# Weight conversion in 512-column pieces, in place, and an FFN that begins at attention step 34

## The chip, the cores and the metric

The kernel runs on one core of one Trainium2 chip. The metric is the device time of one execution in microseconds (us), the median of several runs. The engines are TensorE (PE in the profile; PEld are its weight loads), VectorE (DVE), ScalarE (ACT), GpSimd (POOL) and SyncE (SP), which issues all DMAs here. Each engine works through its own instructions in a fixed order; semaphores tie the engines together.

## The reference

Block-causal attention (8 batches, 8 heads, 576 tokens, head size 64, blocks of 64), then a feed-forward layer over the 4608 tokens:

```python
scores = scale * np.matmul(q, k.transpose(0, 1, 3, 2))
scores = np.where(block_i >= block_j, scores, -1000000000.0)
scores = scores - np.max(scores, axis=-1, keepdims=True)
attn = np.exp(scores)
attn = attn / (np.sum(attn, axis=-1, keepdims=True) + 1e-09)
x = np.matmul(attn, v)                    # then (tokens, heads * head size) = (4608, 512)
h = x @ w_in                              # (4608, 2048)
g = np.where(h >= 1, h, np.where(h <= -1, 0.0, (h + 1) ** 2 / 4))
out = g @ w_out                           # (4608, 512)
```

Queries, keys and values are float32. [...]

## The kernel before

**Numbers.** A float32 operand is split into hi (float32r) and lo = x - hi; a product is hi\*hi + hi\*lo + lo\*hi in float32r passes. Attention times values of batch 0 runs unsplit ("plain").

**Weights.** `convert` (L139) turns a piece of 128 rows of a weight into float32 and splits it. Here a piece has CW = 256 columns, so a weight makes 32 pieces and both make 64. The piece's bits are loaded as pairs of 32-bit words (L147), lower word first. ACT scales the upper word, read as float32 with a step of two words, into the dense tile `work` (L152), and converts the lower word in place (L153). DVE clamps (L154), shifts (L157) and merges the sign (L160), all on the dense `work`. That was the first step; in the second, POOL adds the lower word (L166) and ACT casts to hi (L168); in the third, POOL subtracts hi to get lo (L170). LAG = 2 names those two further steps. Pieces of w_in land in `wih` and `wil`, which stay on chip; pieces of w_out land in `ws`, and when a row block of 512 columns is full it is written to `wo_split` in DRAM, from which the FFN later loads `wo`. `ws` and `wo` share two buffers of the tag "wo". The tiles `bits` and `work` have three buffers each; every other piece below BORROW = 32 uses the FFN's tags "t" and "gl" instead, two buffers each.

**Attention.** 32 pairs of heads (batch by batch, 4 pairs each) run as a software pipeline of eight steps a pair (`attention_steps`, L517): scores by row tiles, softmax (DVE maximum L368, ACT exponential L372, DVE scaling L378; for the last query block L392, L398, L404, in the fourth step), transposes of the probabilities (L418, copied out by L408 and L410), products with the values (L445). An old pair's last products stand in the first two steps of the next one.

**FFN.** Nine chunks of 512 tokens, 16 blocks fc of hidden columns each: 144 units of two half units. `ffn_in` does 12 matmuls into `ph` (L591), then ACT (L600), DVE (L601, L604), ACT (L605) and POOL (L606), and loads `wo`; `ffn_out` does 12 matmuls into `po` (L615, L620).

**The order.** The loop at the end (L659) sets it. At every attention step it starts as many pieces as `want` says: until START = 36 steps a share of EARLY = 24, then more, so that 40 are spread over 24 steps. From START on each attention step is followed by a half unit of the FFN. What is left of the FFN runs after the attention. A scheduler then orders each engine's instructions by their dependencies and a cost model, so that neighbours in the program can stand some places apart on an engine. The memory pools decide how many pieces can be under way.

Of the kernel before, what the change touches and what calls it, by code (L numbers as in the profile page):

```python
# [23 lines left out]
def block_attn_then_ffn(  # L24
# [15 lines left out]
    NTL = S // P                 # whole 128-row tiles of a head  # L40
    SM = NTL * P                 # rows in whole tiles
    QW = SM + 2 * BLK            # query columns of a head: the last block is padded to 128
# [3 lines left out]
    TCH = 512                    # tokens per FFN chunk  # L46
    NCH = NT // TCH
    NTT = TCH // P
    RING = 3 * TCH               # columns of x kept on chip
    G0 = 256                     # query columns of the first attn*v group  # L50
# [4 lines left out]
    BORROW = 32                  # weight pieces among which every other one is converted in  # L55
                                 # buffers of the FFN
    CW = 256                     # columns of a weight that are converted at a time
    F32_TOP = float.fromhex("0x1.dffffcp-96")  # keeps the rounded value finite
    KA = D + NTL                 # contraction rows of hi*hi and the mask
# [7 lines left out]
    conv = ctx.enter_context(tc.tile_pool(name="conv", bufs=3))  # L67
    conv2 = ctx.enter_context(tc.tile_pool(name="conv2", bufs=3))
# [7 lines left out]
    def work_bank(name):  # L76
        # the accumulators' banks serve the attention until the FFN begins
        banks["n"] += 1
        if banks["free"] and banks["n"] % 2:
            return ps_o.tile([P, 512], F32, tag="po", name=name)  # L80
        return ps_w.tile([P, 512], F32, tag="work", name=name)

# [9 lines left out]
    wih = const.tile([P, NCC, DF], F32R, tag="wih", name="wih")  # L92
    wil = const.tile([P, NCC, DF], F32R, tag="wil", name="wil")
    wo_split = dram.tile([NFC, P, 2, DM], F32, tag="wo_split", name="wo_split")

    # Two heads' transposed queries and keys. a: hi rows, then one mask row per whole tile;
    # b: queries hi over lo, keys lo over hi.
# [5 lines left out]
    def last_blocks(t_):  # L103
        """Both heads' last blocks; in the query tiles, head 1's lies behind a block of zeros."""
# [6 lines left out]
    # mask row t: 1 at query block 2t, MASKED at key block 2t + 1  # L111
# [27 lines left out]
    def convert(n, source, hi, lo, done):  # L139
        """CW float64 values, given as bits: their float32, rounded to nearest, in two parts."""  # L140
        if n < BORROW and n % 2:  # in buffers of the FFN
            bits = ffn.tile([P, CW, 2], I32, tag="t", name="bits")
            work = ffn.tile([P, 2, CW], F32, tag="gl", name="work")
        else:
            bits = conv.tile([P, CW, 2], I32, tag="bits", name="bits")
            work = conv2.tile([P, 2, CW], F32, tag="work", name="work")
        nc.sync.dma_start(bits, source.bitcast(I32).rearrange("p (n t) -> p n t", t=2))  # L147
        top, mag = work[:, 0, :], work[:, 1, :].bitcast(U32)
        low = bits[:, :, 0]
        # The upper word, read as float32, has the upper 8 of the 11 exponent bits as its exponent:  # L150
        # times 2^-112 it has the exponent in float32's bias (nothing below 2^-119, and held in range).
        nc.scalar.mul(top, bits[:, :, 1].bitcast(F32), 2.0**-112)  # L152
# [21 lines left out]
    def weight_pieces():  # L174
        """For each piece: its bits, where its parts go, and what follows."""
        for f0 in range(0, DF, CW):
            fs = slice(f0, f0 + CW)
            for cc in range(NCC):
                yield (
                    w_in[cc * P : (cc + 1) * P, fs],  # L180
                    lambda cc=cc, fs=fs: wih[:, cc, fs], lambda cc=cc, fs=fs: wil[:, cc, fs], None,
                )
            for fc in range(f0 // P, (f0 + CW) // P):
                ws = {}

                def part(w, d0, ws=ws):
                    if not ws:
                        ws[0] = ffn.tile([P, 2, DM], F32R, tag="wo", name="ws")
                    return ws[0][:, w, d0 : d0 + CW]

                for d0 in range(0, DM, CW):
                    yield (
                        w_out[fc * P : (fc + 1) * P, d0 : d0 + CW],
                        lambda p_=part, d0=d0: p_(0, d0), lambda p_=part, d0=d0: p_(1, d0),
                        None if d0 + CW < DM else
                        lambda fc=fc, ws=ws: nc.sync.dma_start(wo_split[fc], ws[0].bitcast(F32)),
                    )
# [508 lines left out]
```

## Time and profile before

| what | value |
|---|---|
| median of 3 runs | 1313.78 us (1313.12 to 1313.95) |
| span of the profiled execution | 1305.9 us |
| PE busy | 1234.2 us (95%) |
| DVE busy | 877.9 us (67%) |
| ACT busy | 767.2 us (59%) |
| POOL busy | 462.9 us (35%) |
| mean granted PE clock | 0.978 |

The span runs from the first to the last instruction; the runs' time includes some 8 us around it. The shares are means over the whole span, which has parts of different kinds; so the prediction reads windows of it. In a row of a group, `x` is the count, then follow the busy time in us, the mean of one in ns, and the idle time of the engine just before, with what ended it.

### The profile page before, as it was taken

Reading aid. Unit: us, or ns where it says so; the run is one execution under the profiler, and the core shown is the slowest. Engines: PE = TensorE matmul, PEld = TensorE weight load, DVE = VectorE, ACT = ScalarE, POOL = GpSimd, SP = SyncE. Lnnn points to the kernel's source line nnn. Section 1 sums busy time; section 2 is a strip of 40 time slices with the busy share of each in tenths; the row PEclk is TensorE's granted clock in tenths of the full one; section 3 lists DMA queues with packets and bytes.
Section 4 is the critical chain, followed back from the end, with each engine's and each line's share of the span. In section 5 each row is a group of like instructions: output and inputs, shape, how many; then the busy total and the mean of one; then the engine's idle time right before and its main releaser. Section 6 shows DMA issues by size and latency. Waiting matters only on the chain.

```text
span 1305.9 us, 19727 instructions
## 1 busy us (share of the span) xinstructions
PE 1234.2 (95%) x6496; PEld 1038.7 (80%) x6496; DVE 877.9 (67%) x2200; ACT 767.2 (59%) x1855; POOL 462.9 (35%) x466
## 2 busy tenths in 40 slices
PE   5878777899999999999999999999999999999998
PEld 4666666688888888888888888888888888888886
DVE  8998989867666777776766766676667676322222
ACT  6887676666666666666666666666666565222222
POOL 3554756632233333323333333322333332222221
PEclk9888898999999999999999999999999999999999
DMA  5655454434333433343333432343334322322322
GB/s 153 186 154 167 160 194 159 156 117 131 108 93 104 140 104 97 104 141 106 107 94 103 141 108 85 106 128 104 103 98 137 108 85 63 126 97 97 129 97 97
DMA packets 113766, 156.26 MB, mean 120 GB/s; under 512 B 55920, under 2 KB 72304, under 8 KB 113664
## 3 DMA queue, kind: packets, MB, share of 16 engines
q1 hardware_dynamic: 113664, 155.01, 38.1%
q8 instruction: 51, 0.84, 0.3%
q14 instruction: 51, 0.42, 0.1%
HBM read 120.59 MB, written 17.83 MB: 106 GB/s over the span
## 4 chain that ended last, share of the span: by engine, by line
PE 74%; DVE 12%; ACT 7%; issue 3%; POOL 1%; DMA 1%; SPq 0%; ACTq 0%; POOLq 0%; DVEq 0%
PE ph L591 28%; PE po L615 16%; PE po L620 8%; PE ps_av L445 7%; PE ps_t L418 5%; PE ps_s L345 3%; PE ps_s L348 3%; PE ps_qk L303 3%; DVE pr L378 2%; ACT pr L372 2%; ACT qb L307 2%; DVE nm L368 2%; DVE work L160 1%; DVE work L154 1%; DVE work L157 1%
## 5 line engine op out<-in xcount | busy, mean ns | idle before, releaser
L606 POOL TENSOR_TENSOR gl<-t,gh 128x512 fp32r<-128x512 f32 x144 | 189.6, 1317 | 617.1 <-ACT gh L605 476.0
L615 PE MATMUL po<-wo,gh 128*128 128x512 f32 x1152 | 298.0, 401 | 0.1
L591 PE MATMUL ph<-xh,wih 128*128 128x512 f32 x576 | 240.0, 417 | 1.0 <-DVE sm L354 1.0
L615 PEld LDWEIGHTS po<-wo,gh 128*128 128x128 f32 x1152 | 208.9, 189 | 39.7 <-ACT gh L605 0.5
L601 DVE SCALAR_TENSOR_TENSOR t<-t 128x512 f32<-128x512 f32 x144 | 108.6, 754 | 186.4 <-ACT t L600 186.3
L591 PE MATMUL ph<-xh,wil 128*128 128x512 f32 x576 | 230.7, 401 | 0.0
L591 PE MATMUL ph<-xl,wih 128*128 128x512 f32 x576 | 228.6, 397 | 0.0
L600 ACT ACTIVATE t<-ph 128x512 f32<-128x512 f32 x144 | 86.1, 598 | 167.1 <-PE ph L591 167.1
L372 ACT ACTIVATE pr<-ps_s,nm 128x128 f32<-128x128 f32 (+3 forms) x256 | 134.2, 530 | 58.3 <-DVE nm L368 58.2
L368 DVE TENSOR_REDUCE nm<-ps_s 128x1 f32<-128x128 f32 (+3 forms) x256 | 123.6, 485 | 60.2 <-PE ps_s L348 59.0
L620 PE MATMUL po<-wo,gl 128*128 128x512 f32 x576 | 155.3, 391 | 0.0
L345 PE MATMUL ps_s<-ka,qa 68*128 68x288 f32 (+4 forms) x384 | 124.7, 339 | 21.1 <-ACT pr L372 11.7
L408 ACT CAST pb<-ps_t 128x512 fp32r<-128x512 f32 (+1 forms) x140 | 77.9, 556 | 105.3 <-PE ps_t L418 81.8
L605 ACT CAST gh<-t 128x512 fp32r<-128x512 f32 x144 | 90.2, 626 | 82.3 <-DVE t L604 80.1
L591 PEld LDWEIGHTS ph<-xh,wil 128*128 128x128 f32 x576 | 110.1, 191 | 23.7
L591 PEld LDWEIGHTS ph<-xh,wih 128*128 128x128 f32 x576 | 110.3, 192 | 21.2 <-DVE sm L354 1.5
L591 PEld LDWEIGHTS ph<-xl,wih 128*128 128x128 f32 x576 | 110.9, 192 | 20.5 <-DVE xl L481 0.2
L620 PEld LDWEIGHTS po<-wo,gl 128*128 128x128 f32 x576 | 108.5, 188 | 23.2
L410 DVE TENSOR_TENSOR pb<-ps_t,pb 128x512 fp32r<-128x512 f32 (+1 forms) x140 | 88.3, 631 | 51.1 <-ACT pb L408 51.1
L348 PE MATMUL ps_s<-kb,qb 128*128 128x288 f32 (+4 forms) x384 | 122.3, 325 | 0.0
L418 PE MATMUL ps_t<-ident_r,pr 128*128 128x128 f32 x640 | 108.6, 286 | 7.0 <-DVE x L468 2.2
L378 DVE TENSOR_SCALAR pr<-pr,sm 128x128 f32<-128x128 f32 (+3 forms) x256 | 109.5, 450 | 3.6
(89 smaller groups left out, 2022.2 us busy)
## 6 DMA issues: line engine op xcount, KB each, us to landing
wo<-wo_split SPq DMA_DIRECT2D x144, 512.0 KB, 3.2
out_dram<-ob SPq DMA_DIRECT2D x36, 256.0 KB, 4.5
qn<-in_q_dram SPq DMA_DIRECT2D x32, 256.0 KB, 2.8
kn<-in_k_dram SPq DMA_DIRECT2D x32, 256.0 KB, 2.9
bits<-in_moe_w_in_dram SPq DMA_DIRECT2D x32, 256.0 KB, 2.8
bits<-in_moe_w_out_dram SPq DMA_DIRECT2D x32, 256.0 KB, 2.9
wo_split<-ws SPq DMA_DIRECT2D x16, 512.0 KB, 2.9
qa<-qb SPq DMA_DIRECT2D x63, 128.0 KB, 2.2
```

The lines of the kernel that those rows point to most:

```text
L345: nc.tensor.matmul(ps, qa[:KA, j, c0 : c0 + P], ka[:KA, j, k0 : k0 + n], start=first, stop=False)
L348: nc.tensor.matmul(ps, qb[:, j, c0 : c0 + P], kb[:, j, k0 : k0 + n], start=False, stop=last)
L368: nc.vector.tensor_reduce(out=nm[:, i : i + 1], in_=ps[:, cs], axis=AX.X, op=ALU.max, negate=True)
L372: nc.scalar.activation(pr[:, cs], ps[:, cs], AF.Exp, bias=nm[:, i : i + 1], scale=1.0, accum_out=sm[:, i : i + 1],)
L378: nc.vector.tensor_scalar_mul(pr[:, cs], pr[:, cs], sm[:, i : i + 1])
L418: nc.tensor.transpose(ps[:, c0 : c0 + P], pr[:, c0 : c0 + P], ident)
L445: nc.tensor.matmul(ps[:, lo_col:], vt, x, start=first and i == 0 and m == 0, stop=last and i == len(parts) - 1 and m == len(mov) - 1,)
L591: nc.tensor.matmul(ph, w[:, cc, fs], x[:, cc, xs], start=(cc == 0 and i == 0), stop=(cc == NCC - 1 and i == 2),)
L601: nc.vector.scalar_tensor_tensor(out=t_, in0=t_, scalar=1.0, in1=t_, op0=ALU.min, op1=ALU.mult)
L606: nc.gpsimd.tensor_tensor(out=gl, in0=t_, in1=gh.bitcast(F32), op=ALU.subtract)
L615: nc.tensor.matmul(po[tt], gh[:, ts_], wo[:, w, :], start=(fc == 0 and w == 0), stop=False)
L620: nc.tensor.matmul(po[tt], gl[:, ts_], wo[:, 0, :], start=False, stop=fc == NFC - 1)
```

## The change

A piece has 512 columns, so that both weights make 32 pieces. The upper word is scaled, clamped and kept in `bits`, with a step of two words, and the shifted word goes to a dense tile `mag`. `conv` has two buffers of `bits` and of `mag`, and a pool `early` has two more of each, used by every other piece. w_in is kept in four pairs of tiles of 512 columns; the last pair lies in a pool that is opened in the room of `early` when piece 24 is reached, from which point on only the two `conv` buffers serve. 12 pieces are begun before step 34, then one per step. The FFN begins at step 34 in place of 36. The output tiles `ob` use `conv`'s tags. Comments were taken out as well.

```diff
-    CW = 256                     # columns of a weight that are converted at a time
+    CW = 512
+    NG = DF // CW
...
-    conv = ctx.enter_context(tc.tile_pool(name="conv", bufs=3))
-    conv2 = ctx.enter_context(tc.tile_pool(name="conv2", bufs=3))
+    conv = ctx.enter_context(tc.tile_pool(name="conv", bufs=2))
...
-    wih = const.tile([P, NCC, DF], F32R, tag="wih", name="wih")
-    wil = const.tile([P, NCC, DF], F32R, tag="wil", name="wil")
+    w_in_parts = [
+        [const.tile([P, NCC, CW], F32R, tag=f"wi{x}{g}", name=f"wi{x}{g}") for x in "hl"]
+        for g in range(NG - 1)
+    ]
+    late = {"pool": ctx.enter_context(ExitStack())}
+    late["early"] = late["pool"].enter_context(tc.tile_pool(name="early", bufs=2))
+
+    def open_last_group():
+        late["pool"].close()
+        late["early"] = None
+        last = ctx.enter_context(tc.tile_pool(name="last", bufs=1))
+        w_in_parts.append(
+            [last.tile([P, NCC, CW], F32R, tag=f"wi{x}", name=f"wi{x}") for x in "hl"]
+        )
...
     def convert(n, source, hi, lo, done):
-        if n < BORROW and n % 2:  # in buffers of the FFN
-            bits = ffn.tile([P, CW, 2], I32, tag="t", name="bits")
-            work = ffn.tile([P, 2, CW], F32, tag="gl", name="work")
-        else:
-            bits = conv.tile([P, CW, 2], I32, tag="bits", name="bits")
-            work = conv2.tile([P, 2, CW], F32, tag="work", name="work")
+        pool = late["early"] if n % 2 and late["early"] else conv
+        bits = pool.tile([P, CW, 2], I32, tag="bits", name="bits")
+        mag = pool.tile([P, CW], U32, tag="mag", name="mag")
         nc.sync.dma_start(bits, source.bitcast(I32).rearrange("p (n t) -> p n t", t=2))
-        top, mag = work[:, 0, :], work[:, 1, :].bitcast(U32)
-        low = bits[:, :, 0]
-        nc.scalar.mul(top, bits[:, :, 1].bitcast(F32), 2.0**-112)
+        top, low = bits[:, :, 1].bitcast(F32), bits[:, :, 0]
+        nc.scalar.mul(top, top, 2.0**-112)
         nc.scalar.mul(low, low.bitcast(U32), 2.0**-29)
...
     def weight_pieces():
-        for f0 in range(0, DF, CW):
-            fs = slice(f0, f0 + CW)
+        for g in range(NG):
+            if g == NG - 1:
+                open_last_group()
...
     def ffn_in(c, fc):
-        fs = slice(fc * P, (fc + 1) * P)
+        g, f0 = divmod(fc * P, CW)
+        fs = slice(f0, f0 + P)
+        wih, wil = w_in_parts[g]
...
-            ob = conv.tile([P, DM], F32, tag="bits", name="ob") if tt % 2 else conv2.tile(
-                [P, DM], F32, tag="work", name="ob"
-            )
+            ob = conv.tile([P, DM], F32, tag="bits" if tt % 2 else "mag", name="ob")
...
-    START = 8 * NPAIR + 4        # attention steps before the FFN
-    EARLY = 24                   # conversions before the FFN
+    START = 8 * NPAIR + 2
+    EARLY = 12
...
-        if i < START:
-            want = (i + 1) * EARLY // START
-        else:
-            want = max(
-                EARLY + (i - START + 1) * (NFC // GROUP * PART - EARLY) // (2 * NFC - 4 * GROUP),
-                ((i - START) // (2 * GROUP) + 1) * PART,
-            )
+        want = (i + 1) * EARLY // START if i < START else EARLY + i - START + 1
         want += LAG
```

The pieces come in the same kind of order as before, now by groups of 512 columns of w_in: four pieces of w_in, then the four row blocks of w_out that belong to them. A piece of w_out now fills a whole `ws`.

Two places show how the engines' orders move. First DVE, where the last piece is converted; the names are the program's (`pa`, `pb` are transposed probabilities with their number, `nm` and `sm` the softmax's maximum and sum, `qs`, `ks` the split queries and keys of the next pair). Before, in the fourth step of the eighth pair:

```order
L160 SCALAR_TENSOR_TENSOR work<-work 128x256
L266 SCALAR_TENSOR_TENSOR qs<-qn,qs 128x9x64
L601 SCALAR_TENSOR_TENSOR t<-t 128x512
L368 TENSOR_REDUCE nm<-ps_s 128x1
L604 TENSOR_TENSOR t<-ph,t 128x512
L410 TENSOR_TENSOR pa_3002<-ps_t,pa_3001 128x384
L354 TENSOR_SCALAR sm<-sm 128x1
L275 CAST ks<-kn 128x64
L355 RECIPROCAL sm<-sm 128x1
L378 TENSOR_SCALAR pr<-pr,sm 128x512
L392 TENSOR_REDUCE nm<-ps_s 128x1 x2
L396 TENSOR_TENSOR nm<-nm 128x1
```

Now, in the fourth step of the seventh pair (L162, L165, L168 are the old L154, L157, L160; L403, L411, L610 the old L396, L404, L601):

```order
L165 TENSOR_SCALAR mag<-bits 128x512
L403 TENSOR_TENSOR nm<-nm 128x1
L417 TENSOR_TENSOR pb_2289<-ps_t,pb_2288 128x3x128
L168 SCALAR_TENSOR_TENSOR mag<-bits,mag 128x512
L409 TENSOR_TENSOR sm<-sm 128x1
L361 TENSOR_SCALAR sm<-sm 128x1
L362 RECIPROCAL sm<-sm 128x1
L411 TENSOR_SCALAR pr<-pr,sm 128x576
L610 SCALAR_TENSOR_TENSOR t<-t 128x512
```

The last conversion stands one pair of heads, eight steps, earlier in the program; 12 FFN units' L601 stand ahead of it before, 9 of L610 now.

Second POOL, among the later pieces (`vs` are split values, `gl` is the FFN's lo part). Before:

```order
L166 TENSOR_TENSOR work<-work,bits 128x256
L170 TENSOR_TENSOR ws<-work,ws 128x256 x2
L166 TENSOR_TENSOR work<-work,bits 128x256 x2
L170 TENSOR_TENSOR ws<-work,ws 128x256 x2
L170 TENSOR_TENSOR wil<-work,wih 128x256
L606 TENSOR_TENSOR gl<-t,gh 128x512
```

Now, in the last group (L174 and L178 are the old L166 and L170, L615 the old L606):

```order
L174 TENSOR_TENSOR mag<-mag,bits 128x512
L615 TENSOR_TENSOR gl<-t,gh 128x512
L178 TENSOR_TENSOR wil<-mag,wih 128x512
L174 TENSOR_TENSOR mag<-mag,bits 128x512
L299 TENSOR_TENSOR vs_2293<-vn,vs_2293 128x4x64
L299 TENSOR_TENSOR vs_2293<-vn,vs_2293 64x64
L178 TENSOR_TENSOR wil<-mag,wih 128x512
```

Adds of two pieces no longer stand side by side here: with two buffers, an add is followed by the subtraction of the piece before it.

More of the change, by code (lines that the diff above doesn't have):

```diff
@@ L54, in block_attn_then_ffn @@
     EPS = 1e-9
-    BORROW = 32
-    CW = 256
+    CW = 512
+    NG = DF // CW
     F32_TOP = float.fromhex("0x1.dffffcp-96")
@@ L174, in weight_pieces, with part @@
     def weight_pieces():
-        for f0 in range(0, DF, CW):
-            fs = slice(f0, f0 + CW)
+        for g in range(NG):
+            if g == NG - 1:
+                open_last_group()
             for cc in range(NCC):
                 yield (
-                    w_in[cc * P : (cc + 1) * P, fs],
-                    lambda cc=cc, fs=fs: wih[:, cc, fs], lambda cc=cc, fs=fs: wil[:, cc, fs], None,
+                    w_in[cc * P : (cc + 1) * P, g * CW : (g + 1) * CW],
+                    *(lambda cc=cc, part=part: part[:, cc, :] for part in w_in_parts[g]), None,
                 )
-            for fc in range(f0 // P, (f0 + CW) // P):
+            for fc in range(g * CW // P, (g + 1) * CW // P):
                 ws = {}
-                def part(w, d0, ws=ws):
+                def part(w, ws=ws):
                     if not ws:
                         ws[0] = ffn.tile([P, 2, DM], F32R, tag="wo", name="ws")
[L189 to L196, printed above, removed]
-                    )
+                    return ws[0][:, w, :]
+                yield (
+                    w_out[fc * P : (fc + 1) * P, :],
+                    lambda p_=part: p_(0), lambda p_=part: p_(1),
+                    lambda fc=fc, ws=ws: nc.sync.dma_start(wo_split[fc], ws[0].bitcast(F32)),
+                )
     def prepare_weights():
@@ L647, in feed_forward @@
         yield
-    START = 8 * NPAIR + 4
-    GROUP = CW // P
-    PART = NCC + GROUP * DM // CW
-    EARLY = 24
+    START = 8 * NPAIR + 2
+    EARLY = 12
     LAG = 2
@@ L659, in block_attn_then_ffn @@
     for i, _ in enumerate(attention_steps()):
-        if i < START:
-            want = (i + 1) * EARLY // START
-        else:
-            want = max(
-                EARLY + (i - START + 1) * (NFC // GROUP * PART - EARLY) // (2 * NFC - 4 * GROUP),
-                ((i - START) // (2 * GROUP) + 1) * PART,
-            )
+        want = (i + 1) * EARLY // START if i < START else EARLY + i - START + 1
         want += LAG
```

## Prediction

> **What bounds the kernel now.** I read the 40 slices first, then the windows, then the groups of each engine in two stretches.
>
> ```profile
> span 1305.9 us, 19727 instructions
> ...
> PE   5878777899999999999999999999999999999998
> ...
> DVE  8998989867666777776766766676667676322222
> PEclk9888898999999999999999999999999999999999
> ...
> 0.00:105.00 105.00, 76.53 (x404) 61.99 (x404) 91.22 (x272) 82.94 (x226) 49.54 (x67) 0.92 0.56 164
> 105.00:258.00 153.00, 121.85 (x571) 96.85 (x571) 138.92 (x319) 103.53 (x281) 97.21 (x111) 0.89 0.51 166
> 258.00:1105.00 847.00, 840.31 (x4654) 718.59 (x4654) 592.09 (x1527) 531.57 (x1267) 269.33 (x252) 1.00 0.36 109
> ...
> 1105.00:1205.00 100.00, 100.00 (x453) 82.95 (x453) 29.60 (x48) 26.40 (x47) 23.66 (x19) 1.00 0.29 100
> ```
>
> The window rows give the busy time of PE, weight load, DVE, ACT and POOL, then PE's clock. There are two regimes. From 258 us on PE is busy 99% and more: nothing that other engines save there counts. Up to 258 us, where the last weight piece is converted, DVE is busy 230.1 of 258 us (0.892), PE has gaps and a granted clock of about 0.9. The change lies in this first regime, and what it is worth is the time by which the regime ends sooner, less the PE work that it then leaves over.
>
> ```profile
> L160 DVE SCALAR_TENSOR_TENSOR work<-work 128x256 uint32<-128x256 uint32 x64 | 34.9, 550 | 0.5
> L154 DVE TENSOR_SCALAR work<-work 128x256 f32<-128x256 f32 x64 | 29.4, 464 | 7.9 <-ACT work L152 7.7
> L157 DVE TENSOR_SCALAR work<-work 128x256 uint32<-128x256 uint32 x64 | 27.7, 440 | 0.5
> L378 DVE TENSOR_SCALAR pr<-pr,sm 128x512 f32<-128x512 f32 x14 | 12.0, 854 | 0.1
> L601 DVE SCALAR_TENSOR_TENSOR t<-t 128x512 f32<-128x512 f32 x12 | 11.2, 936 | 0.6 <-ACT t L600 0.5
> L378 DVE TENSOR_SCALAR pr<-pr,sm 128x384 f32<-128x384 f32 x15 | 10.8, 717 | 0.1
> ...
> L378 DVE TENSOR_SCALAR pr<-pr,sm 128x256 f32<-128x256 f32 x15 | 8.3, 555 | 0.0
> ...
> L378 DVE TENSOR_SCALAR pr<-pr,sm 128x128 f32<-128x128 f32 x15 | 7.7, 515 | 0.1
> L604 DVE TENSOR_TENSOR t<-ph,t 128x512 f32<-128x512 f32 x11 | 7.5, 679 | 0.0
> ```
>
> These are DVE's groups of 0 to 258 us (busy us, mean ns). Conversion takes 92.0 us of DVE, all else 138.1. The same forms from 300 to 1100 us, where POOL does little, are shorter:
>
> ```profile
> L601 DVE SCALAR_TENSOR_TENSOR t<-t 128x512 f32<-128x512 f32 x93 | 70.1, 754 | 52.5 <-ACT t L600 52.5
> ...
> L378 DVE TENSOR_SCALAR pr<-pr,sm 128x512 f32<-128x512 f32 x46 | 22.0, 479 | 0.8
> ...
> L378 DVE TENSOR_SCALAR pr<-pr,sm 128x384 f32<-128x384 f32 x46 | 19.1, 415 | 0.8
> ...
> L378 DVE TENSOR_SCALAR pr<-pr,sm 128x256 f32<-128x256 f32 x46 | 16.0, 347 | 0.0
> ...
> L378 DVE TENSOR_SCALAR pr<-pr,sm 128x128 f32<-128x128 f32 x46 | 13.1, 284 | 1.4
> ```
>
> So beside a busy POOL a DVE instruction on SBUF is held up: 854 for 479 ns, 936 for 754.
>
> **Part 1, wider pieces on DVE.** Two old pieces cost 2 x (550 + 464 + 440) = 2908 ns. A new one has three instructions of 512 columns. A tensor_scalar gains 132 ns from 256 to 512 columns without POOL (479 - 347) and 299 beside it (854 - 555): L154 becomes 596 to 763, L157 572 to 739; I take the middles, 680 and 655. The third lies between 754 and 936; I take 880, nearer the row of this stretch. Sum 2.22 us, ends 1.92 and 2.44: 32 pieces take 71.0 us for 92.0.
>
> **Part 2, longer POOL instructions.** POOL's conversion groups up to 262 us:
>
> ```profile
> L166 POOL TENSOR_TENSOR work<-work,bits 128x256 int32<-128x256 int32 x64 | 53.4, 838 | 66.5 <-DVE work L160 11.3 <-ACT bits L153 9.5 <-ACT pr L372 7.9
> L170 POOL TENSOR_TENSOR wil<-work,wih 128x256 fp32r<-128x256 f32 x32 | 27.1, 848 | 8.8 <-ACT wih L168 8.2 <-DMA vn<-in_v_dram 0.5
> ...
> L606 POOL TENSOR_TENSOR gl<-t,gh 128x512 fp32r<-128x512 f32 x12 | 16.6, 1381 | 17.4 <-ACT gh L605 15.6 <-DMA kn<-in_k_dram 1.5 <-DVE work L154 0.2
> ```
>
> At 512 columns one lasts as L606's 1381 ns: 64 make 88 us where 128 made 106. POOL is busier with each and less in total. The attention's scaling (L378) is held (854 - 479) x 14 + (717 - 415 + 555 - 347 + 515 - 284) x 15 = 16.4 us in this stretch. If waits follow the length of a POOL instruction (1381/840, 1.6 times) this grows by 10 us; if they follow POOL's total they grow by nothing. I take 6. [...] The rows agree that DVE is held (854 for 479 ns), not how the hold grows.
>
> **Part 3, where the conversions end.** The first pair of rows on DVE's order, in the part on the change, shows it: before, the last conversion stands in the fourth step of the eighth pair, with 12 FFN units (L601) ahead; now in the fourth step of the seventh, with 9 ahead. So conversion ends 8 attention steps and 3 FFN units (6 half units) sooner in the program: this comes from the denser schedule, one piece of 512 columns a step for 40/24 x 256, and from the start two steps earlier, which moves the FFN's first unit, its matmuls, its two DVE instructions and its wo load on SP, ahead of two attention steps. What leaves the DVE-bound stretch:
>
> ```profile
> L160 DVE SCALAR_TENSOR_TENSOR work<-work 128x256 uint32<-128x256 uint32 x40 | 23.1, 586 | 0.4
> L157 DVE TENSOR_SCALAR work<-work 128x256 uint32<-128x256 uint32 x39 | 19.8, 516 | 0.3
> ...
> L154 DVE TENSOR_SCALAR work<-work 128x256 f32<-128x256 f32 x39 | 17.1, 446 | 1.7 <-ACT work L152 1.6
> ```
>
> From 105 to 258 us (24 steps) DVE spends 138.9 - 60.0 = 78.9 us beside conversion, of it 12 x (936 + 679) ns = 19.4 on FFN units and 59.5 on attention, 2.48 a step. Eight steps are 19.8 us, three units 4.8. The stretch then holds 138.1 - 24.6 = 113.5, + 71.0, + 6 = 190.5 us of DVE; at 0.892 it ends at 213.6, 44.4 us sooner.
>
> What PE must still do comes back on the path. The last-block activations mark the pairs:
>
> ```profile
> L398 ACT ACTIVATE pr<-ps_s,nm x50: 492/503/512, 262.7 to 1094.2; 128x288 f32<-128x288 f32 x50
> ```
>
> Two a pair, 25 pairs: 831.5/24 = 34.6 us for 8 steps with 8 half units. A half unit is 12 matmuls, 12 x 100/453 = 2.65 us. Eight steps and six halves are 34.6 - 5.3 = 29.3 us. **Sum:** -44.4 + 29.3 = -15.1 us. On the profiled span that is 1290.8; 7.9 us lie between the span and the median of 1313.78, so 1298.7. With 1.92 us and no more waits it is 1281, with 2.44 and 10 it is 1311.
>
> **Part 4, at nothing.** ACT's conversion instructions and the loads halve in number; both lie behind DVE (ACT is busy 186 of 258 us), and without that cover less ACT work could only gain. The last group's tiles lie where the early buffers were, so the first cast of the 25th piece waits for POOL's subtraction of the 24th: once, at most one POOL instruction, 1.4 us, with the softmax behind it on ACT. Output tiles have two and two buffers for three and three; a chunk needs four and comes every 16 x 2 half units, 85 us at 2.65 each, so they are free.
>
> **Rivals.** *Strided DVE (slower).* The upper word stays in bits, so DVE reads every second word in all three instructions and writes so in one. No DVE row has a step of two. The nearest has a step of four, against a dense one:
>
> ```profile
> L309 DVE CAST qa<-ps_qk x1: 1046/1046/1046, 10.9 to 10.9; 64x512 fp32r<-64x512 f32 x1
> L309 DVE CAST ka<-ps_qk x1: 1084/1084/1084, 12.0 to 12.0; 64x512 fp32r<-64x512 f32 x1
> ...
> L630 DVE COPY ob<-po 128x512 f32<-128x512 f32 x12 | 8.2, 685 | 1.4 <-PE po L620 1.4
> ...
> L152 ACT ACTIVATE work<-bits 128x256 f32<-128x256 f32 x64 | 28.0, 439 | 13.6 <-DMA bits<-in_moe_w_in_dram 8.0 <-POOL ws L170 4.3 <-DMA bits<-in_moe_w_out_dram 1.3
> L153 ACT ACTIVATE bits<-bits 128x256 int32<-128x256 uint32 x64 | 27.9, 444 | 1.0 <-DMA bits<-in_moe_w_in_dram 0.5 <-DMA bits<-in_moe_w_out_dram 0.4
> ...
> L168 ACT CAST wih<-work 128x256 fp32r<-128x256 f32 x32 | 12.9, 409 | 17.5 <-POOL work L166 17.3
> ...
> L307 ACT CAST kb<-ps_qk 128x512 fp32r<-128x512 f32 x16 | 17.8, 1114 | 0.3 <-PE ps_qk L303 0.3
> ...
> L408 ACT CAST pb<-ps_t 128x512 fp32r<-128x512 f32 x9 | 5.4, 602 | 1.3 <-PE ps_t L432 1.3
> ```
>
> Step four costs DVE 380 ns (mean 1065 - 685). At that price three instructions add 1.14 us a piece, 36.5 us, 41 on the path: 1340. At half of it 1319. The midpoint, 0.85 us a piece, gives 1329; from 0.42 us a piece on (15.1 x 0.892/32) the change is no gain. Against it: on ACT step four (L307) costs 512 ns over L408, but step two (L152, L153) only 30 to 35 over L168, and POOL's L166, with one operand of step two, is no longer than L170. I keep step two at nothing in the sum. [...]
>
> *Buffers (about the same).* After 24 pieces only two bits buffers are left, and ws shares two wo buffers with the FFN's wo, now with four ws in a row. POOL's rows on the change show the result: one piece's add (L174) stands between subtractions (L178), where before two adds often stood together.
>
> ```profile
> wo<-wo_split SPq DMA_DIRECT2D x144, 512.0 KB, 3.2
> ```
>
> A piece holds its bits for a landing of this size, 3.2 us, two ACT passes of at most 2 x 2 x 0.44, 2.2 of DVE and 1.38 of POOL: 8.5 us. Two buffers pass one piece per 4.3 us, and a step takes 153/24 = 6.4. If queueing doubles the 8.5, each of the last 8 pieces comes 2.1 us late, 17 us in all; behind its load on SP stand qa<-qb and the loads of q and k, and on ACT, which waits in order, the softmax. Taken at 13: 1312. That it stays hidden is likelier: before, ACT waited 4.3 us for a buffer in all (<-POOL ws L170, in L152's row).
>
> *Late start (the change doesn't do what it says).* Step 33, counted from 0, makes the last x of batch 0, so a start at 34 may wait for it.
>
> ```profile
> L600 ACT ACTIVATE t<-ph x144: 582/599/635, 115.6 to 1294.8; 128x512 f32<-128x512 f32 x144
> ```
>
> The first unit's activation is at 115.6 us; if it stays there, the two half units (5.3 us) come back: 1304. Against it, each step here lasts only 105/36 = 2.9 us, so that the wait is short.
>
> **How the numbers follow.** Sum 0.55 (1299, own range 1281 to 1311), strided 0.20 (1329), buffers 0.17 (1312), late start 0.08 (1304). A difference below 0.2% (2.6 us) can't be told from none. Faster: 0.53 + 0.08 + 0.04 = 0.65; same: 0.02 + 0.07 = 0.09; slower: 0.20 + 0.06 = 0.26. The range, 1284 to 1326, leaves out the lowest of the sum and half of the strided case.
>
> **What would show it.** Right: the three DVE conversion groups near 0.68, 0.66 and 0.88 us; L411 of the seventh pair near 218 us, and PE without gaps behind it; then 34.6 us a pair as before. Strided: DVE's groups above 0.9 us, and 1.2 for the third. Buffers: ACT or DVE waiting for bits' DMA or for wo in the last 8 pieces. Late start: the first activation on ph no sooner than 115 us. The forecast is wrong if DVE's share of the first stretch falls well below 0.89, so that something else sets its end.

## The result and the profile after

| | before | after |
|---|---|---|
| median on the same chip | 1313.57 us (1313.12 to 1313.95, 4 runs) | 1334.84 us (1334.38 to 1336.1, 4 runs) |
| span of the profiled execution | 1305.9 us | 1332.8 us |
| DVE busy, first 236 us | 211.75 us | 198.41 us |

The ratio is 1.0165, 95% interval 1.0151 to 1.0179: the change makes the kernel 21 us slower. The forecast was 1299 us with a range up to 1326, so its direction is wrong. Executions of the kernel before, taken beside the experiments, last 1307.5 to 1314.5 us, and its profiled one is by its span among the short ones, so that differences from that trace can hide up to some 5 us of a gain.

The page of the changed kernel: the span, the slices, and two of the groups of ffn_in's matmuls (busy us, mean ns, idle time just before).

```profile
span 1332.8 us, 19398 instructions
...
PE   4877787999999999999999999999999999999998
...
DVE  7888978766666676666676666677776676422222
...
PEclk9788888999999999999999999999999999999999
...
L600 PE MATMUL ph<-xh,wih 128*128 128x512 f32 x576 | 239.3, 416 | 6.3 <-ACT xh L517 3.6
L600 PE MATMUL ph<-xl,wih 128*128 128x512 f32 x576 | 230.2, 400 | 11.8 <-POOL xl L518 9.2
```

New here are the releasers L517 and L518, the store of x into the ring. The conversions, in the groups of DVE and POOL from 0 to 270 us of the same kernel:

```profile
L168 DVE SCALAR_TENSOR_TENSOR mag<-bits,mag 128x512 uint32<-128x512 uint32 x32 | 27.3, 857 | 0.2
L162 DVE TENSOR_SCALAR bits<-bits 128x512 f32<-128x512 f32 x32 | 22.5, 707 | 6.2 <-issue 3.8 <-ACT bits L160 2.4
L165 DVE TENSOR_SCALAR mag<-bits 128x512 uint32<-128x512 uint32 x32 | 21.0, 661 | 5.6 <-POOL ws L178 3.5 <-POOL wil L178 1.5
...
L174 POOL TENSOR_TENSOR mag<-mag,bits 128x512 int32<-128x512 int32 x32 | 44.4, 1389 | 66.2 <-ACT bits L161 17.9 <-DVE mag L168 16.3 <-issue 12.8
```

Conversion costs DVE 27.3 + 22.5 + 21.0 = 70.8 us, against 92.0 before. That saving is there, and the kernel is slower all the same.

To see where, I take the start of the last block's first exponential (L398 before, L405 after) in each pair of heads and subtract before's. The same table for five of the experiments below:

| us later than before, at pair | 5th | 7th | 8th | 9th | 13th | 17th | 21st | 25th | 29th | 32nd | end of span |
|---|---|---|---|---|---|---|---|---|---|---|---|
| after (FFN at 34) | 10.0 | 19.5 | 6.6 | 10.7 | 15.7 | 20.7 | 27.5 | 28.4 | 31.7 | 31.2 | 26.9 |
| after, FFN at 36 | 8.0 | 12.0 | -1.4 | -1.0 | -1.0 | -0.6 | -0.6 | -0.3 | -0.2 | -0.2 | 0.1 |
| before, FFN at 34 | 1.1 | 3.9 | 3.9 | 7.5 | 12.4 | 17.4 | 22.3 | 23.2 | 27.9 | 27.4 | 23.0 |
| after, FFN at 35 | 7.6 | 14.1 | 3.7 | 4.8 | 8.1 | 11.4 | 14.7 | 16.3 | 19.7 | 20.6 | 16.9 |
| after, x stored in two parts | 9.2 | 20.4 | 7.5 | 11.3 | 15.9 | 20.7 | 21.6 | 22.4 | 23.2 | 22.6 | 17.4 |
| before without the limit | 1.8 | -0.9 | -3.8 | -4.6 | -4.5 | -4.5 | -4.5 | -4.5 | -4.5 | -4.5 | -4.8 |

The change loses 6.6 us up to the eighth pair and 24.6 behind it, in steps against the pair before of 4 to 7 us at the 9th, 13th, 17th, 21st and 29th pair (1.5 at the 25th), and gets 4.3 back at the end, where two half units fewer are left. Each step lies where an FFN chunk begins. PE's waits in that stretch (262 to 1130 us; total us, times, longest), of the change, then of before:

```profile
PE ph L600 <- POOL xl L518: 8.6, 5, 1.8
PE ps_qk L310 <- ACT pr L379: 8.2, 24, 0.8
PE ph L600 <- ACT xh L517: 3.6, 5, 0.8
```

```profile
PE ps_qk L303 <- ACT pr L372: 5.1, 17, 0.3
```

At five chunk starts PE waits 0.7 us for xh and some 1.7 us for xl. That is 12.2 us of 24.6. The windows of the 24 pairs show the rest (columns: PE, weight load, DVE, ACT, POOL busy, clock, DMA share, GB/s), first of the change, then of before:

```profile
269.20:1124.90 855.70, 835.36 (x4586) 709.96 (x4585) 586.74 (x1495) 525.12 (x1246) 260.92 (x247) 0.99 0.36 105
```

```profile
262.70:1093.70 831.00, 825.57 (x4584) 705.92 (x4583) 579.00 (x1495) 523.09 (x1245) 265.13 (x248) 1.00 0.36 109
```

Of 24.7 us, 14.9 are idle (20.34 for 5.43) and 9.8 are PE being busy longer with as many matmuls. At the chunk of the 21st pair, in windows of the change:

```profile
728.00:730.00 2.00, 0.72 (x3) 0.41 (x3) 1.08 (x4) 1.05 (x3) 1.95 (x2) 1.00 0.65 142
730.00:732.00 2.00, 1.13 (x4) 0.83 (x4) 1.10 (x1) 0.00 (x0) 0.81 (x1) 0.55 0.57 164
732.00:734.00 2.00, 2.00 (x7) 1.61 (x6) 1.19 (x3) 0.97 (x2) 0.00 (x0) 0.50 0.43 122
734.00:736.00 2.00, 2.00 (x7) 1.52 (x6) 0.57 (x1) 0.00 (x0) 0.00 (x0) 0.50 0.00 0
736.00:738.00 2.00, 2.00 (x11) 1.76 (x10) 1.50 (x3) 1.25 (x3) 0.00 (x0) 0.74 0.00 0
738.00:740.00 2.00, 2.00 (x13) 1.74 (x13) 1.20 (x3) 0.92 (x2) 1.29 (x1) 1.00 0.94 364
```

In two gaps that together make 2.5 us PE's granted clock falls to 0.5 and stays low for 6.8 us: 7 matmuls in 2 us where 13 run at clock 1.00. So this chunk cost 6 to 7 us and not 2.5. The clock records of the trace have such a fall at the chunks of the 13th, 17th and 21st pair (3.4, 3.4 and 6.8 us at 0.50), which cost 5.2, 4.9 and 6.4 us measured to the pair before the next chunk; at the 9th and the 29th the clock stays at 1.00, and the chunk costs 3.4 to 3.8 us. So of the 24.6 us 12.2 are waits for x and at most 6.8, half of the 13.7 us at 0.50, are the clock; the rest is other waits (PE's for L379 grew from 5.1 to 8.2 us) and busy time that I can't assign.

### The profile page after: what moved, and what is told of

Same layout as the page of the kernel before. It is cut to its first block, busy times and chain, and to the rows that moved or that the text cites. A ratio compares the mean times of both kernels' runs of the same rounds, so it can differ in the third digit from the quotient of the medians.

```text
span 1332.8 us, 19398 instructions
## 1 busy us (share of the span) xinstructions
PE 1246.1 (93%) x6496; PEld 1046.2 (78%) x6496; DVE 872.0 (65%) x2104; ACT 760.6 (57%) x1759; POOL 443.6 (33%) x402
## 5 line engine op out<-in xcount | busy, mean ns | idle before, releaser
L615 POOL TENSOR_TENSOR gl<-t,gh 128x512 fp32r<-128x512 f32 x144 | 189.3, 1314 | 642.6 <-ACT gh L614 505.4
L624 PE MATMUL po<-wo,gh 128*128 128x512 f32 x1152 | 303.9, 406 | 0.1
L624 PEld LDWEIGHTS po<-wo,gh 128*128 128x128 f32 x1152 | 213.0, 193 | 41.8 <-ACT gh L614 0.5
L610 DVE SCALAR_TENSOR_TENSOR t<-t 128x512 f32<-128x512 f32 x144 | 106.9, 742 | 189.2 <-ACT t L609 189.2
L379 ACT ACTIVATE pr<-ps_s,nm 128x128 f32<-128x128 f32 (+3 forms) x256 | 133.7, 526 | 61.7 <-DVE nm L375 61.5
L375 DVE TENSOR_REDUCE nm<-ps_s 128x1 f32<-128x128 f32 (+3 forms) x256 | 123.7, 486 | 64.5 <-PE ps_s L355 63.4
L385 DVE TENSOR_SCALAR pr<-pr,sm 128x128 f32<-128x128 f32 (+3 forms) x256 | 111.0, 456 | 3.9
```

Of the source, the lines that this page charges most:

```text
L375: nc.vector.tensor_reduce(out=nm[:, i : i + 1], in_=ps[:, cs], axis=AX.X, op=ALU.max, negate=True)
L379: nc.scalar.activation(pr[:, cs], ps[:, cs], AF.Exp, bias=nm[:, i : i + 1], scale=1.0, accum_out=sm[:, i : i + 1],)
L385: nc.vector.tensor_scalar_mul(pr[:, cs], pr[:, cs], sm[:, i : i + 1])
L610: nc.vector.scalar_tensor_tensor(out=t_, in0=t_, scalar=1.0, in1=t_, op0=ALU.min, op1=ALU.mult)
L615: nc.gpsimd.tensor_tensor(out=gl, in0=t_, in1=gh.bitcast(F32), op=ALU.subtract)
L624: nc.tensor.matmul(po[tt], gh[:, ts_], wo[:, w, :], start=(fc == 0 and w == 0), stop=False)
```

## The experiments

Line numbers are the change's, moved by a line or two where a line was added. "Ratio" is to the kernel before on the same chip.

**The FFN's start and the conversions apart.** The change with the FFN at 36, and before with it at 34:

```diff
+    FFN_AT = 36          # in the change;  34 in the kernel before
-        if i >= START:
+        if i >= FFN_AT:
```

> The changed kernel with the FFN put back to step 36; the pieces are begun at the same steps as in the changed kernel (12 before step 34, then one a step). Theory: at step 34 the FFN's chunks 1 to 6 come to x just after its last part is made, and PE waits at each chunk (from pair 7 on the pair marks fall back by 24.6 us, with PE gaps behind L517 and L518). With two steps more between them the waits go and two half units (about 5.4 us) come back at the end: 1334.8 - 24.6 + 5.4 = 1316 us, no PE gap behind the store of x. Rival (the conversions, with their size and few buffers, make the whole loss): the time stays above 1328.

> The kernel before with the FFN begun at step 34 and nothing else changed (pieces begun at the same steps, 256 columns). Theory (waits on x at each chunk): 1313.6 + 24.6 - 5.4 = 1333 us, with PE gaps behind the store of x (L510, L511) at chunks 1 to 6. Rival (the conversions make the loss): 1308 to 1314, since two half units are done two steps sooner.

Measured: 1307.75 us, ratio 0.9962 (0.9949 to 0.9975), and 1334.74 us, ratio 1.0163 (1.0137 to 1.019). The start alone reproduces the whole loss, on the old conversion too; the conversion and its schedule alone are a gain of 0.4%. The run at 36, the changed conversion with the old start, is faster than both kernels. That gain rests on the medians: the two profiled executions have nearly one span (1306.0 and 1305.9 us). At a start of 34 the new conversion gains nothing over the old one (ratios 1.0165 and 1.0163).

**Slower conversions.** With the FFN at 36, 12 pieces until step 36 and the other 20 over 24 steps, as dense in columns as before:

```diff
-        want = (i + 1) * EARLY // START if i < START else EARLY + i - START + 1
+        want = (i + 1) * 12 // 36 if i < 36 else 12 + (i - 35) * 20 // 24
```

> As e1, and the pieces are spread as before the change: 12 of 512 columns until step 36, then 20 over 24 steps in place of one a step. If the dense schedule and the buffers behind it hold up the first stretch (pair marks 10 us late at pair 4, 17 to 20 at pairs 5 and 6), it is 5 to 10 us faster than e1. If the spreading is of no account, it is within 3 us of e1. If dense is better, because fewer steps are bound by DVE, it is slower than e1 by 5 us or more.

Measured: 1313.1 us, ratio 1.0009 (0.9998 to 1.002). So the denser schedule is worth some 5 us, and the wide pieces without it nothing that can be told from none, although they shorten DVE's part of the conversion just as much.

**A pause of two half units.** The change, with no half unit at steps 64 and 65, ahead of the second chunk:

```diff
+    HOLD = (64, 65)
-            next(ffn_steps, None)
+            if i not in HOLD:
+                next(ffn_steps, None)
```

> The changed kernel, FFN from step 34, but with no half unit at steps 64 and 65, so that from chunk 1 on it stands to the attention as a start at 36 does; the first stretch is that of the changed kernel to the instruction. Theory (waits on x at chunks 1 to 6): 1316 us and no gap behind the store of x at chunks 1 to 6. What it differs by from e1 is what the start at 34 does to the first stretch alone: if e1 is lower by 3 us or more, the early start also delays the attention before step 60. Rival (conversions): above 1328.

Measured: 1312.58 us, ratio 1.0007 (0.9994 to 1.002), its last pair 4.0 us later than before's in place of 31.2. So the repeated meeting makes most of the loss. What is left against the run at 36, 4.8 us on the same chip, is what the early start does to the first stretch: the eighth pair comes 6.1 us later than before's here and 1.4 us sooner there. In its waits of the same stretch no row names the store of x:

```profile
PE ps_qk L310 <- ACT pr L379: 5.9, 19, 0.6
PE ps_s L352 <- ACT kb L314: 0.5, 1, 0.5
```

**The store of x in two parts**, the FFN still at 34: the first 256 columns a step earlier.

```diff
             if old:
+                old.store_x(0, G0)
                 old.turn(1, 2)
             yield
...
-                old.store_x()
+                old.store_x(G0, S)
```

> The changed kernel, the FFN still at step 34, but x is stored in two parts: its first 256 columns at the first step of the next pair, as soon as they are added, the other 320 one step later where all 576 were stored. Of batch c the chunk c needs 512 - 64c columns: chunks 4 to 6 need only the first part, chunk 2 the part up to 384, chunks 1 and 3 the 320 columns as well. Theory (the wait for x): no wait at chunks 2, 4, 5, 6, a shorter one (about 1.4 us in place of 2.5, by 320 of 576 columns of the two instructions) at 1 and 3; of the 24.6 us that the pairs lose between the eighth pair and the last, 4 to 8 remain: 1314 to 1320 us. Rival (the wait is not what costs): 1330 to 1336 us.

Measured: 1325.15 us, ratio 1.0103 (1.0077 to 1.0128). The waits that are left:

```profile
PE ps_qk L310 <- ACT pr L379: 8.3, 24, 0.7
PE ph L600 <- POOL xl L517: 4.2, 3, 1.5
PE ph L600 <- ACT xh L516: 2.2, 3, 0.8
```

Three waits in place of five: those of chunks 4 and 6 are gone, and from the 21st pair on the steps are 1.4 us. The size was missed: at chunks 1, 2 and 3, where chunk 2 was to have none, the two waits together still take 2.1 us for 2.4, (4.2 + 2.2)/3, and cost 4 to 5 us as before. The store's length is the smaller part of that delay; the other is when x comes to be. The change itself holds the same test: where a batch wraps around the ring, L518 already goes in two parts.

```profile
L518 POOL TENSOR_TENSOR xl<-x,xh x36: 589/1464/1890, 171.6 to 1150.1; 128x576 fp32r<-128x576 f32 x20, 128x384 fp32r<-128x384 f32 x8, 128x192 fp32r<-128x192 f32 x8
```

Batch 5 begins at column 2880 - 1536 = 1344 of 1536, so its first 192 columns are stored first, and chunk 5 needs just 6 x 512 - 2880 = 192 of it: the 25th pair is the one without a wait. Batch 2 is stored in two parts as well, 384 columns first, and chunk 2 needs all 384; they reach past the first 256 of x, and there the wait stays (1.6 us for xl).

**The FFN at 35, 37, 38 and 40**, with the change's piece steps.

> The changed kernel with the FFN begun at step 35 (34 in the change, 36 in the run that came out at 1307.8 us), the conversions at the change's own steps. Theory (TensorE waits for the last x of a batch): at 34 it reaches x about 2.5 us before ScalarE and GpSimd have stored it; one more step of attention and one half unit lie between at 35, some 4.3 us, so the wait at each chunk is gone: 1306 to 1310 us, and no wait of ph for L517 or L518 above 0.5 us. Rival (the FFN at 34 costs by its earlier need of converted weights and by its own work beside the conversions, step by step): halfway between 1307.8 and 1334.8, about 1321 us.

> The changed kernel with the FFN begun at step 37. At 35 no wait for x was left, yet the pairs behind the conversions took 35.4 us in place of 34.6, and three scalings on VectorE (L272 twice, L385 once a pair) that take 0.18 to 0.41 us at 36 took 0.95 to 1.42 us, each ending with a subtraction of GpSimd. Theory (an odd step puts the FFN's subtractions of GpSimd beside these scalings, whatever the distance): the same at 37, the pairs at 35.4 us, 1319 to 1325 us. Rival (at 35 the FFN was still too near to the attention): 1306 to 1311 us.

> The changed kernel with the FFN begun at step 38. Theory (two half units fewer beside the conversions shorten the first stretch, since VectorE bounds it: from 34 to 36 the eighth pair came 8.0 us sooner, for 5.3 us of two half units behind the attention): once more, 1304 to 1307 us. Rival (at 36 the stretch is bound by the conversions' own steps, and the two half units are only put off): 1307.8 + 5.3, about 1313 us.

> As the run at step 38, with the FFN begun at 40. Theory: four half units less in the first stretch, each pair of them 2.7 us to the good: 1301 to 1306 us. Rival: four half units put off, 1318 us. In between where the stretch stops being bound by VectorE.

Measured: at 35 1324.81 us, ratio 1.0101 (1.008 to 1.0123); at 37 1326.11, 1.012 (1.0095 to 1.0145); at 38 1312.21, 1.0005 (0.9993 to 1.0017); at 40 1318.23, 1.0058 (1.0036 to 1.0081).

At 35 the wait for x is gone as the theory said, and the time is lost to something that neither theory had. The scaling of the queries from 300 to 1100 us (ns as least/median/most), at 35, then at 36:

```profile
L272 DVE TENSOR_SCALAR qs<-qn x44: 951/978/1427, 328.9 to 1072.8; 128x512 fp32r<-128x512 f32 x22, 128x64 fp32r<-128x64 f32 x22
```

```profile
L272 DVE TENSOR_SCALAR qs<-qn x44: 178/296/410, 322.0 to 1050.5; 128x512 fp32r<-128x512 f32 x22, 128x64 fp32r<-128x64 f32 x22
```

A piece of the timeline at 35 (start, duration in us):

```profile
469.29 1.29 POOL L615 TENSOR_TENSOR gl<-t,gh 128x512 fp32r<-128x512 f32 x1 [6.74 <-ACT gh L614]
469.38 1.41 DVE L385 TENSOR_SCALAR pr<-pr,sm 128x384 f32<-128x384 f32 x1
...
470.54 0.85 POOL L299 TENSOR_TENSOR vs<-vn,vs 128x256 fp32r<-128x256 f32 x1
...
470.72 2.29 DVE L272 TENSOR_SCALAR qs<-qn 128x512 fp32r<-128x512 f32 x2
...
471.35 1.60 POOL L518 TENSOR_TENSOR xl<-x,xh 128x576 fp32r<-128x576 f32 x1
```

L385 starts 0.09 us behind POOL's L615 and ends 0.21 us behind its end; the two L272 behind it end 0.3 and 0.1 us behind the two POOL instructions that follow (L299 and L518). With an odd start the subtractions of POOL and the scalings of DVE coincide, in every pair, and a pair takes 35.3 us ((1114.8 - 266.4)/24, with the second exponential of the last pair) for 34.7. Step 37 shows the same within 3 ns (951/977/1424), which settles that it is the phase and not the distance. Steps 38 and 40 are free of both. There the eighth pair comes at -4.0 and -9.0 us against before, after -1.4 at 36, but two half units put off behind the attention cost some 5.5 us each time by the spans, and the lead melts on the way (-1.0 and -0.3 at the last pair), in part by PE's waits for L379 (7.3 and 9.7 us for 5.6 at 36): the theory that expected a gain was wrong, and 36 is the best of the six starts.

**What the first stretch gives for less work.** Four runs, all with the FFN at 36: ACT's cast a step later, the load a step earlier, one early buffer for two, and 16 early pieces for 12.

```diff
+        yield                                  # ahead of the cast's  w32 = w32.bitcast(F32)
...
+        yield                                  # behind the load of bits
...
-    ... tc.tile_pool(name="early", bufs=2)
+    ... tc.tile_pool(name="early", bufs=1)
...
-    EARLY = 12
+    EARLY = 16
```

In the first two LAG is 3.

> The changed kernel with the FFN at 36 (1307.8 us) and, besides, ScalarE's cast of a piece's upper part one step behind GpSimd's addition that it waits for (a conversion then takes 3 steps after its first in place of 2). Theory (in the first stretch ScalarE stands in order behind the cast of a 512-column piece, which waits for an addition of 1.39 us, and the attention's exponentials stand behind it: 10.7 us of such waits up to 125 us of the span, 8.1 us from there to 235 us): these waits go, the seventh pair comes 5 to 10 us sooner, 1298 to 1303 us. Rival (VectorE's queue sets the stretch, ScalarE's waits lie beside it): within 2 us of 1307.8; or slower, if the buffers that are held a step longer delay the next loads: 1312 us or more.

> The changed kernel with the FFN at 36 (1307.8 us) and, besides, each piece's load issued one step ahead of its first conversion (a conversion then takes 3 steps after its load in place of 2). Theory (the first stretch is late because a load of 512 KB takes 4.1 to 4.6 us to land, of which no step is left between load and use): the pairs up to the seventh come 3 to 8 us sooner, 1300 to 1305 us. Rival (ScalarE waited only about 1 us for loaded bits in that kernel up to 125 us of the span, so the loads were mostly hidden): within 2 us of 1307.8.

> The changed kernel with the FFN at 36 (1307.8 us) and one buffer in the room of the last group in place of two, so that a piece in it is loaded only when the piece two before it is done. Theory (the added buffers carry the conversions of 512 columns: a load takes 4.1 to 4.6 us to land and a conversion two steps): every second piece of the first 24 is late by 2 to 4 us, ScalarE waits for its bits, and the first stretch grows: 1318 to 1345 us. Rival (VectorE bounds the stretch and covers it): 1306 to 1311 us.

> The changed kernel with the FFN at 36 and 16 pieces in place of 12 in the first 34 steps, so that the last piece starts four steps sooner. Theory (in the first five pairs VectorE is idle 15% of the time, some 19 us, which more pieces fill, and the stretch with FFN and conversions becomes shorter): the fifth pair 2 to 4 us later, the eighth 3 to 6 us sooner, 1302 to 1305 us. Rival (a piece costs the same wherever it stands, or more among the first pairs): 1307 to 1312 us.

Measured: 1310.11 us, ratio 0.9992 (0.9979 to 1.0006); 1310.01, 0.9991 (0.998 to 1.0002); 1311.24, 1.0007 (0.9994 to 1.002); 1311.43, 1.0001 (0.999 to 1.0012). None gains: by their spans (1308.4, 1307.1, 1307.4 and 1309.5 us) they lie 1 to 4 us above the run at 36 (1306.0), by their ratios 4 to 6. So neither the cast's wait, nor the landing of a load, nor room for more pieces alone sets the stretch. The first two edits also hold a piece's buffers a step longer, which can have hidden a small gain. The added buffer is worth a few us and not the 10 to 37 that the first theory asked for.

Last, the price of DVE's time: the limit left out, on before and on the change with the FFN at 36.

```diff
-        nc.vector.tensor_scalar(
-            out=top, in0=top, scalar1=F32_TOP, scalar2=-F32_TOP, op0=ALU.min, op1=ALU.max
-        )
```

> The kernel before without the first of the three VectorE instructions of a conversion (the limit at the largest finite value is left out): 64 of the 128 instructions of 452 ns, 28.9 us less on VectorE up to the eighth pair. Theory of the prediction (VectorE sets the first stretch, and a microsecond off it is about a microsecond of time): the eighth pair 22 to 30 us sooner, until TensorE bounds it; 1285 to 1295 us. Rival (the chain from scores over maxima, exponentials and transposes sets it, with VectorE's queue as only one part): the eighth pair 5 to 15 us sooner, 1298 to 1308 us.

> The changed kernel with the FFN at 36 (1307.8 us) and the same instruction left out: 32 of 652 ns, 20.9 us less on VectorE. Theory of the prediction: the eighth pair 15 to 21 us sooner, 1288 to 1294 us. Rival (the 512-column pieces have already taken VectorE off the path, and its idle time grows): within 5 us, 1303 to 1308 us.

Measured: 1304.42 us, ratio 0.9941 (0.9926 to 0.9956), and 1304.49, 0.9938 (0.9922 to 0.9953). The first 236 us of before, then of before without the limit:

```profile
0.00:236.00 236.00, 181.15 (x894) 144.83 (x895) 211.75 (x550) 172.72 (x468) 133.18 (x161) 0.90 0.54 168
```

```profile
0.00:236.00 236.00, 182.09 (x899) 147.04 (x900) 187.69 (x492) 172.71 (x468) 129.67 (x164) 0.88 0.55 168
```

DVE is busy 24.1 us less, and PE has done 0.9 us more. The profiled spans, 1305.9 and 1301.1 us, differ by 4.8, and the ratio gives 7.7: a microsecond off DVE is worth 0.2 to 0.3. On the change it is 3.5 us (spans 1306.0 and 1302.5) for 20.9 us of instructions, hardly 0.2. The eighth pair of before came 3.8 us sooner, less than either theory had.

## Why the prediction was wrong

**The conversion's cost (part 1) was right.** 2.22 us a piece were forecast as 0.68 + 0.655 + 0.88; measured are 0.71 + 0.66 + 0.86. The rival of the strided operands falls with it: 26 of the 32 L168, with a step of two in their first operand, take 668 to 694 ns, the dense L610 mostly 691 (its median over the run), and 22 of the 32 L162, which also writes with that step, 404 to 434, for 406 to 410 of the dense L272 of 512 columns and 479 of L378. The means of the conversion are higher through the other instructions of these groups, 24 of 96 with those of L165, which last 710 to 2682 ns; each of the 24 overlaps one of POOL's.

```profile
L162 DVE TENSOR_SCALAR bits<-bits x32: 404/428/2682, 12.3 to 229.8; 128x512 f32<-128x512 f32 x32
L168 DVE SCALAR_TENSOR_TENSOR mag<-bits,mag x32: 668/682/1918, 13.2 to 235.2; 128x512 uint32<-128x512 uint32 x32
```

That size was read rightly, its worth was not. The rows of groups count overlapping durations: those of 0 to 258 us of before add up to 265.6 us, shape by shape, where the window has DVE busy for 230.1, so 92.0 may not be taken out of 230.1. From the start to the eighth pair DVE's busy time fell by 12.2 us (234.77 to 222.59, one FFN unit more), not by 21.

**Longer waits for POOL (part 2, 6 us) hardly came.** The durations of DVE's instructions over the first eight pairs sum to 272.0 us before and 252.3 after: 19.7 less for a conversion that is 21.8 less in the same sum, with one FFN unit more (1.6 us).

**"At 0.892 it ends at 213.6" (part 3) failed.** The step took DVE's share for a bound that stays. The last L168 begins at 235.2 us, before's last L160 at 255.5: not 44.4 but some 20 us sooner. Up to 236 us DVE is busy 198.4 us, where the sum had 190.5, and its share is 0.84 for 0.90:

```profile
0.00:236.00 236.00, 176.38 (x827) 142.46 (x828) 198.41 (x444) 159.94 (x367) 121.06 (x106) 0.86 0.55 169
```

The two runs without the limit show why: DVE's time there has a price of 0.2 to 0.3, not 1/0.892. By this price 21 us are worth 4 to 6, and the change with the FFN at 36 gained 5.0 by its ratio; but as the wide pieces on the old schedule gained nothing, this agreement is luck and not a confirmation. In the run at 36 the fifth pair is 8 us late, the seventh 12, and the time returns when the conversions end; why wide pieces delay the first pairs is not settled, since neither fewer of them early (14 for 16 by step 36), nor the later cast, the earlier load or the missing limit, nor the start at 35, brought the fifth pair to less than 7 us. That DVE is 90% busy was read rightly; that it sets the end was only inferred. What sets it stays open: without the limit DVE is busy 0.80, PE 0.77, ACT 0.73, so no engine alone; a chain that runs from one to the other would look so, but I did not isolate it. One count was off as well: by their starts 11 of L601 and not 12 lie ahead of before's last L160, the next 1 us behind it, for 9 of L610.

**The start at 34, "which moves the FFN's first unit", is the failed step that decided.** I charged it with instructions moved and with one wait, in the case of the late start: 5.3 us, once, at a chance of 0.08. I saw that step 33 makes the last x of batch 0, but not that a chunk has 32 half units and a batch 32 steps, so that every chunk meets the last x of its batch at the same distance. The first chunk shows it already: the first unit waits for the last values of batch 0 behind DVE's queue, as in all five kernels that start at 34 or 35 and in none that starts later, and its activation comes even later than the 115.6 us that I had named as the sign (the first start in the second row, both of the change):

```profile
PE ph L600 <- DVE xl L488: 2.6, 1, 2.6
```

```profile
L609 ACT ACTIVATE t<-ph x144: 583/597/601, 122.1 to 1322.0; 128x512 f32<-128x512 f32 x144
```

So the late start was right in kind and wrong in size. The waits of some 2.4 us came at five more chunks, 12.2 us, and at three of these the clock added up to 6.8. The run with the pause, which takes these meetings away and leaves the start, came out level with the kernel before (1.0007 for 1.0165).

**The regime behind the conversions was right but not safe.** Away from the chunk starts a pair takes 34.7 us as before. "Nothing that other engines save there counts" held; that nothing which they delay counts was never said, and there lay the loss: PE at 99% has no slack, so each wait is paid in full.

**The buffers** showed their sign in part: from 180 to 250 us ACT waits 4.8 us for the loads of bits (L160), and DVE 5.0 us for POOL to leave a buffer of mag (L165 behind L178). What the two buffers of the last pieces cost in time no run isolates; one early buffer fewer cost 1.5 us by the spans and 5.9 by the ratios. **Span and median**: the 7.9 us added between them are not a fixed cost, as the change's profiled execution took 1334.57 us with a span of 1332.8.

## What to carry to other kernels

When one stage is moved against another that it feeds on, look for the period of both: if they are equal, a wait at the first meeting recurs at all of them, and its price is the sum. A busy share of 0.9 names a suspect for the bound; leaving out one known instruction tells the price of its time before a saving is multiplied by it. And where an engine is full, ask of an edit what it makes late there, not only what it saves elsewhere.

## What the runs showed of the hardware

**The clock answers to short gaps, and on a fixed grid.** In the change's trace all sixteen falls of the granted clock to 0.50 begin at whole multiples of 3.41 us from each other, and but for the one at the end they last one, two or three such steps; the twelve falls of before's trace lie on a grid of the same step and last as long, again but for the one at the end. Windows along this grid tell the chunks apart. At the 9th pair the two gaps lie across an edge, and PE is busy 2.39 and 1.92 of 3.41 us; at the 13th both lie in one window, it is busy 1.08, and the next window runs at 0.50:

```profile
296.71:300.12 3.41, 2.39 (x11) 1.43 (x9) 2.65 (x7) 1.86 (x5) 2.79 (x3) 1.00 0.34 78
300.12:303.54 3.42, 1.92 (x9) 1.58 (x10) 1.95 (x4) 1.11 (x4) 1.45 (x2) 1.00 0.64 175
303.54:306.95 3.41, 3.41 (x22) 3.02 (x21) 3.27 (x7) 1.81 (x4) 0.41 (x1) 1.00 0.23 83
440.07:443.48 3.41, 1.08 (x4) 0.51 (x4) 1.37 (x3) 0.76 (x2) 3.28 (x5) 1.00 0.64 151
443.48:446.90 3.42, 3.42 (x10) 2.63 (x10) 1.84 (x5) 2.02 (x5) 0.29 (x1) 0.50 0.35 108
446.90:450.31 3.41, 3.41 (x21) 3.06 (x20) 2.64 (x6) 1.43 (x4) 1.29 (x1) 1.00 0.18 68
```

The 17th and 21st pair go with the 13th (busy 1.47 and 1.55 us, then 0.50), the 29th with the 9th (2.71 and 1.71 us, clock 1.00). Over the windows at clock 1.00 of the traces of before and of the change, from 30 to 1290 us, the clock fell behind each of the 10 in which PE was busy for less than 0.4 of the time, and behind none of the 659 over 0.7; between these it fell behind 16 of 29. At the 13th pair two gaps of 0.8 and 1.6 us inside one window were enough.

**A scaling on DVE can last until POOL's subtraction ends.** The scalings of the queries (L272), 0.18 to 0.41 us with the FFN at 36, took 0.95 to 1.43 us at 35, and there L385, begun at 469.38 us, ended 0.21 us behind L615. In the change all seven L385 of 512 columns that began inside an L518 or L615, 0.3 us or more before its end, took 1.12 to 1.51 us and ended 0.28 to 0.29 us behind it; the same scaling of before (L378) has a mean of 0.48 from 300 to 1100 us. Not every operation is held: a maximum over 512 columns of scores (L375), begun at 120.68 us of the change inside POOL's L283 of 1.42 us, took its usual 0.68. Nor is every scaling: L385 of 384 columns, begun at 297.39 us of the change inside POOL's L299 of 1.20 us, took 0.41. New to me was the consequence: shifting a stage by one step changed nothing in the amount of work and cost 17 us (spans of 1322.8 and 1306.0 us).
